# Decode attention over two caches: the last softmax maximum ahead of a PV product, and V stationary for B's last two PV products

## The chip, the cores and the metric

The kernel runs on one core of a Trainium2 chip. The metric is device microseconds of one execution, given as the median of several runs. Beside these runs there is one execution recorded by the hardware profiler; all durations of single instructions come from it.

## What is computed

Two independent attention blocks, A and B, each for one new token with 32 heads of 128 elements. A attends over its whole cache of 16384 positions, B only over the last 4096 positions of its cache. The two output rows of 512 are put side by side.

```python
q = (x @ wq).reshape(B, Sq, Hq, Dh)           # x: 1 x 512, 32 heads of 128
# B alone: k, v = the last W = 4096 positions of the caches
scores = jnp.einsum("bhqd,bhkd->bhqk", q, k) * (Dh ** -0.5)
p = _softmax(scores, axis=-1)
o = jnp.einsum("bhqk,bhkd->bhqd", p, v)
return o.transpose(0, 2, 1, 3).reshape(B, Sq, Hq * Dh) @ wo    # 4096 x 512
```

All inputs and the output are bf16. Every cached key and value is used once, by one query, so that nearly all of the traffic is K and V read once from HBM.

## The kernel before, in words

**Tiles and steps.** There are 20 steps T (`steps`, `NT`), 16 of A and 4 of B. The B steps are T = 0, 7, 13 and 19; step 18 is the last of A and step 19, the last of all, is B. An A step takes two heads: their 2 x 16384 positions lie on 128 partitions, 256 positions each. A B step takes eight heads as two groups of four, 128 positions on each partition for either group. Each step is walked in two halves, u = 0 and u = 1. For A a half is half of the positions of the pair, for B a half is a group of its own. A `Unit` is what has a softmax of its own: an A pair, or one B group.

**Scores.** These are made on VectorE, in place in the K tile: `scores_prod` (L194) multiplies K by the query, `scores_tree` halves the 128 products by additions (L201) and ends with a reduction (L207).

**Softmax.** `unit_max` takes a maximum on each partition (L212) and transposes it on TensorE (L214). `max_all` takes the maximum for each head on VectorE (L219, L223) and spreads it by a matmul (L226). `soft` makes the bias and the exponentials on ScalarE (L231, L234), the sums of the exponentials on TensorE (L241 or L246), and spreads the probabilities into `pm`, one masked copy for each head (L253). `recip` takes the reciprocal of the sums on VectorE. For a unit with `un.last` the sum comes out on all 128 partitions, with the heads as columns (L240, L241, L261), otherwise on a few rows (L246, L263).

**PV.** `pv` (L275) is 32 matmuls for a half: the probabilities are the stationary operand (128 x 8 for A, 128 x 16 for B), four positions of V, 512 elements, move past them. The result has 4 rows for each head, of which `evict` (L291, ScalarE) makes a scaled copy, `columns` (L306, eight matmuls) adds the four slices into columns, and L310 writes them to `s.O`. `pv_columns` (L317) does the same in another manner: V of one position is the stationary operand (128 x 128), the heads' probabilities move (4 columns), 128 matmuls in all, and the result is already in columns; one VectorE instruction (L321) scales it and writes `s.O`. Before the change only the last group, (19, 1), uses it.

**Output.** `permute_o` puts the 32 columns of O in the order of wo's rows, `project_out_columns` (L345) multiplies 128 blocks of wo, each stationary, by one column of O each, and `store_out` transposes, casts and stores. B's wo comes in five pieces of 16, 8, 4, 2 and 2 of its 32 row blocks (`wo_pieces`), and the products of a piece follow those of the one before.

**Queues and order.** The order on each engine is the order in which the code is written out. All loads of K, V and the weights go through SyncE's one DMA queue, in the order of the code, and a load whose tile is still read waits there. The V ring has two slots. At the end its tiles are V(18,0), V(18,1), V(19,0) and B's wo, so that B's wo takes the slot of V(18,1) and can be requested only when `pv(18, 1)` has read it. A's wo and V(19,1) share a slot of the K ring. At the last two turns of the loop, x = 38 and 39, and behind the loop the order is, in short:

```python
# x = 38: ... pv(17, 1); load_v(18, 1); pv(18, 0); scores_tree(19, 0) ... unit_max(19, 0)
# x = 39: load_v(19, 0); load_v(19, 1, W); columns(); scores_prod(19, 1)
#         max_all + soft of (19, 0); pv(18, 1); load_wo(B)
#         scores_tree(19, 1); recip; evict(); unit_max(19, 1)
# behind: columns(); max_all + soft + recip of (19, 1); pv(19, 0); evict(); columns()
#         permute_o(A); project_out_columns(A); store_out(A)
#         pv_columns(19, 1); permute_o(B); project_out_columns(B); store_out(B)
```

Of the kernel before, what the change touches and what calls it, by code (L numbers as in the profile page):

```python
# [10 lines left out]
BF16 = mybir.dt.bfloat16  # L11
P = 128
# [5 lines left out]
CH = 128  # L18
# [7 lines left out]
def kernel(  # L26
# [37 lines left out]
    def vslot(name):  # L64
        return vring.tile([P, CH, DH], BF16, tag="vring", name=name)
# [74 lines left out]
    def load_wo(s, W, pieces):  # L140
        s.wo_t = W.rearrange("p a b -> p (a b)").rearrange("p (r f) -> p r f", r=HQ)
        src = s.wo.rearrange("(p r) f -> p r f", r=HQ)
        r = 0
        for n in pieces:
            nc.sync.dma_start(out=s.wo_t[:, r : r + n, :], in_=src[:, r : r + n, :])
            r += n
# [31 lines left out]
    class Unit:  # L178
        def __init__(self, T, u):
            self.T = T  # L180
            self.s, g = steps[T]
            self.col = self.s.nh * g if self.s is A else self.s.nh * (2 * g + u)
            self.n = 2 * CH if self.s is A else CH
            self.rows = 4 * self.s.nh
            self.last = T == NT - 1 and u == 1
            self.sc = one.tile([P, 2 * CH], F32, tag="sc", name="sc")

    units = {}
# [39 lines left out]
    def soft(un):  # L228
        s = un.s
        bias = small.tile([P, 1], F32, tag="bias", name="bias")  # L230
        nc.scalar.activation(out=bias[:, :], in_=un.sm[:, 128:129], func=ACT.Copy, scale=-inv)  # L231
        p = one.tile([P, 2 * CH], BF16, tag="p", name="p")
        cs = small.tile([P, 1], F32, tag="cs", name="cs")
        nc.scalar.activation(  # L234
            out=p[:, 0 : un.n], in_=un.sc[:, 0 : un.n], func=ACT.Exp, scale=inv, bias=bias[:, :],
            accum_out=cs[:, :],
        )
        if un.last:
            csm = small.tile([P, 4], F32, tag="csm", name="csm")
            nc.scalar.activation(out=csm[:, 0 : s.nh], in_=s.mask[:, :], func=ACT.Copy, scale=cs[:, :])  # L240
            nc.tensor.matmul(  # L241
                un.sm[:, 136 : 136 + s.nh], lhsT=ones_col[:, :].broadcast_to([P, P]), rhs=csm[:, 0 : s.nh],
                start=True, stop=True,
            )
        else:
            nc.tensor.matmul(  # L246
                un.sm[0 : un.rows, 136:137], lhsT=s.rows[:, :, :].rearrange("p a b -> p (a b)"), rhs=cs[:, :],
                start=True, stop=True,
            )
        pm = small.tile([P, 4 * CH], BF16, tag="pm", name="pm")  # L250
        un.pm = pm[:, 0 : un.n * s.nh].rearrange("p (i h c) -> p i h c", h=s.nh, c=4)
        for j in range(s.nh):
            nc.scalar.activation(  # L253
                out=un.pm[:, :, j, :], in_=p[:, 0 : un.n].rearrange("p (i c) -> p i c", c=4),
                func=ACT.Copy, scale=s.mask[:, j : j + 1],
            )

    def recip(un):
        un.r = small.tile([P, 4], F32, tag="r", name="r")
        if un.last:  # L260
            nc.vector.reciprocal(un.r[:, 0 : un.s.nh], un.sm[:, 136 : 136 + un.s.nh])  # L261
        else:
            nc.vector.reciprocal(un.r[0 : un.rows, 0:1], un.sm[0 : un.rows, 136:137])  # L263
# [3 lines left out]
    def pv(T, u):  # L267
        s = steps[T][0]
        un = units[T, u if s is B else 0]
        first, final = (True, True) if s is B else (u == 0, u == 1)  # L270
        if first:
            un.o = ps_o.tile([16, 512], F32, tag="o", name="o")
        i0 = u * CH // 4 if s is A else 0
        for i in range(CH // 4):
            nc.tensor.matmul(  # L275
                un.o[0 : un.rows, :],
                lhsT=un.pm[:, i0 + i, :, :].rearrange("p a b -> p (a b)"),
                rhs=V[T, u][:, 4 * i : 4 * i + 4, :],
                start=(first and i == 0),
                stop=(final and i == CH // 4 - 1),  # L280
            )
        if final:
            ready.append(un)
# [3 lines left out]
    def evict():  # L287
        while ready:
            un = ready.pop(0)
            un.osb = one.tile([16, 512], F32, tag="o4", name="o4")  # L290
            nc.scalar.activation(  # L291
                out=un.osb[0 : un.rows, :], in_=un.o[0 : un.rows, :], func=ACT.Copy,
                scale=un.r[0 : un.rows, 0:1],
            )
            evicted.append(un)
            if ready:
                columns()

    def columns():
        while evicted:  # L300
            un = evicted.pop(0)
            s, n = un.s, un.rows
            oc = ps_s.tile([P, 4], F32, tag="sp", name="oc")
            sel = identf[0:n, 0:n].rearrange("k (h c) -> k c h", c=4)
            for j in range(4):
                nc.tensor.matmul(  # L306
                    oc[:, 0 : s.nh], lhsT=un.osb[0:n, j * P : (j + 1) * P], rhs=sel[:, j, :],
                    start=(j == 0), stop=(j == 3),
                )
            nc.scalar.copy(s.O[:, un.col : un.col + s.nh], oc[:, 0 : s.nh])  # L310

    def pv_columns(T, u):
        un = units[T, u]
        s = un.s
        o = ps_o.tile([P, 4], F32, tag="o", name="ocol")
        for l in range(CH):
            nc.tensor.matmul(  # L317
                o[:, 0 : s.nh], lhsT=V[T, u][:, l, :], rhs=un.pm[:, l // 4, :, l % 4],
                start=(l == 0), stop=(l == CH - 1),
            )  # L320
        nc.vector.tensor_tensor(  # L321
            out=s.O[:, un.col : un.col + s.nh], in0=o[:, 0 : s.nh], in1=un.r[:, 0 : s.nh], op=ALU.mult
        )
# [50 lines left out]
    with tc.manual_schedule():  # L374
        for s in (B, A):
            nc.scalar.dma_start(out=s.xT[:, :], in_=s.x[0, 0, :].rearrange("(p c) -> p c", c=KC))
        scratch = kslot("scratch")
        new_k(0)
        load_wq(B)
        load_k(0, 0)  # L380
        load_wq(A)
        load_k(0, 1)
        make_identity(nc, identf[:, :])
        nc.vector.memset(one_f[:, :], 1.0)
        nc.vector.memset(ones_col[:, :], 1.0)
        nc.vector.tensor_copy(ident[:, :], identf[:, :])
        spread_x(B, scratch[:, :, :].rearrange("p a b -> p (a b)"))
        for s in (B, A):
            make_masks(s)
        nc.vector.memset(pick[:, :], 0.0)  # L390
        nc.vector.tensor_copy(
            pick[:, 4 : 4 + P].rearrange("h (m k) -> h m k", k=4)[:, :, 0], identf[0:HQ, 0:HQ]
        )
        spread_x(A, one.tile([P, 2 * KC * P], BF16, tag="o4", name="xbA")[:, :])
        project_q(B)
        project_q(A)
        new_k(1)
        load_k(1)
        done = None
        for x in range(2 * NT):  # L400
            T, u = divmod(x, 2)
            if u == 0 and T >= 1:
                load_v(T - 1, 0)
                if T + 1 < NT:
                    new_k(T + 1)
                    load_k(T + 1)
            if x == 2 * NT - 2:
                W = kslot("wot")
                load_wo(A, W[:, 0:CH, :], (HQ,))
            if x == 2 * NT - 1:  # L410
                load_v(T, 0)
                load_v(T, 1, W[:, CH : 2 * CH, :])
            columns()
            scores_prod(T, u)
            if done is not None:
                max_all(done)
                soft(done)
            if u == 0 and T >= 1:
                if T >= 2:
                    pv(T - 2, 1)  # L420
                load_v(T - 1, 1)
                pv(T - 1, 0)
            if x == 2 * NT - 1:
                pv(T - 1, 1)
                load_wo(B, vslot("wot")[:, :, :], wo_pieces)
            nxt = scores_tree(T, u)
            if done is not None:
                recip(done)
            evict()
            done = nxt  # L430
            if done is not None:
                unit_max(done)
        columns()
        max_all(done)
        soft(done)
        recip(done)
        pv(NT - 1, 0)
        evict()
        columns()
        permute_o(A)  # L440
        project_out_columns(A, (HQ,))
        store_out(A)
        pv_columns(NT - 1, 1)
        permute_o(B)
        project_out_columns(B, wo_pieces)
        store_out(B)
# [30 lines left out]
```

## Time and profile before

| what | value |
|---|---|
| median of 3 runs | 836.62 us (834.75 to 836.89) |
| the profiled execution, its own time | 833.46 us |
| its span, first to last instruction | 831.7 us |
| mean granted TensorE clock | 0.704 |
| VectorE busy | 761.0 us (92%) |
| TensorE matmul busy | 394.2 us (47%) |
| ScalarE busy | 67.8 us (8%) |
| read from HBM | 352.32 MB, 424 GB/s over the span |

The span leaves out 1.76 us of the profiled execution's time that lies before its first and behind its last instruction. Positions such as "at 792.62" are microseconds from the start of the span. "Granted clock" is the share of TensorE's full speed that the throttle gave. In the tables of the profile, PE is TensorE's matmuls, PEld its weight loads, DVE is VectorE, ACT ScalarE, and SPq the DMA requests that SyncE issues; "issue" is time in which an engine waited for nothing that the profile shows.

### The profile page before, as it was taken

Reading aid. Unit: us, or ns where it says so; the run is one execution under the profiler, and the core shown is the slowest. Engines: PE = TensorE matmul, PEld = TensorE weight load, DVE = VectorE, ACT = ScalarE, POOL = GpSimd, SP = SyncE. Lnnn points to the kernel's source line nnn. Section 1 sums busy time; section 2 is a strip of 40 time slices with the busy share of each in tenths; the row PEclk is TensorE's granted clock in tenths of the full one; section 3 lists DMA queues with packets and bytes.
Section 4 is the critical chain, followed back from the end, with each engine's and each line's share of the span. In section 5 each row is a group of like instructions: output and inputs, shape, how many; then the busy total and the mean of one; then the engine's idle time right before and its main releaser. Section 6 shows DMA issues by size and latency. Waiting matters only on the chain.

```text
span 831.7 us, 4818 instructions
## 1 busy us (share of the span) xinstructions
PE 394.2 (47%) x2012; PEld 171.9 (21%) x2012; DVE 761.0 (92%) x356; ACT 67.8 (8%) x196; POOL 0.7 (0%) x6
## 2 busy tenths in 40 slices
PE   3515061808263453638081635536371808163677
PEld 1102020303021221213030212112120303021236
DVE  1899999999999999999999999999999999999910
ACT  0011010100000011101010000111010101000111
POOL 0000000000000000000000000000000000000000
PEclk9666576758585867667585958676676758595886
DMA  9999999999999999999999999999999999999994
GB/s 378 429 435 461 409 455 405 450 419 432 448 414 432 428 448 416 442 426 439 424 443 419 445 421 430 442 422 445 418 449 416 442 424 444 416 432 432 430 426 173
DMA packets 10694, 352.64 MB, mean 424 GB/s; under 512 B 1456, under 2 KB 1456, under 8 KB 1840
## 3 DMA queue, kind: packets, MB, share of 16 engines
q1 hardware_dynamic: 10376, 352.33, 98.4%
q8 instruction: 16, 0.26, 0.1%
q10 hardware_dynamic: 296, 0.00, 0.0%
q14 instruction: 6, 0.05, 0.0%
HBM read 352.32 MB, written 0.00 MB: 424 GB/s over the span
## 4 chain that ended last, share of the span: by engine, by line
DVE 79%; DMA 15%; PE 5%; issue 1%; ACT 1%; DVEq 0%; ACTq 0%
DVE kt L194 36%; DVE kt L201 35%; DMA kt<-in_A_k_cache_dram 10%; DVE sc L207 5%; PE o L275 3%; DMA xTA<-in_A_x_dram 3%; DMA vt<-in_A_v_cache_dram 2%; PE out_cols L345 1%; DVE m L212 1%; DVE Mr L223 1%; DVE M L219 0%; PE ocol L317 0%; PE oc L306 0%; ACT o L291 0%; DVE r L263 0%
## 5 line engine op out<-in xcount | busy, mean ns | idle before, releaser
L201 DVE TENSOR_TENSOR kt<-kt 128x8192 bf16<-128x8192 bf16 (+3 forms) x160 | 344.9, 2156 | 4.7
L275 PE MATMUL o<-vt,pm 128*8 128x512 bf16 (+1 forms) x1248 | 316.0, 420 | 9.9 <-DMA vt<-in_A_v_cache_dram 9.9
L194 DVE TENSOR_TENSOR kt<-kt,qA 128x16384 bf16<-128x16384 bf16 x32 | 277.5, 8672 | 2.9 <-DMA kt<-in_A_k_cache_dram 2.9
L275 PEld LDWEIGHTS <-pm 128*8 128x8 bf16 (+1 forms) x1248 | 116.2, 94 | 199.8 <-issue 72.5
L214 PE MATMUL sm<-identf,m 128*1 128x128 f32 x24 | 8.4, 350 | 196.5 <-DVE m L212 196.4
L226 PE MATMUL sm<-one_f,Mr 1*128 1x1 f32 x48 | 13.1, 340 | 177.4 <-DVE Mr L223 177.4
L194 DVE TENSOR_TENSOR kt<-kt,qB 128x16384 bf16<-128x16384 bf16 x8 | 69.5, 8681 | 0.0
L207 DVE TENSOR_REDUCE sc<-kt 128x128 f32<-128x1024 bf16 x40 | 48.8, 1220 | 2.9
L226 PEld LDWEIGHTS sm<-one_f,Mr 1*128 1x128 f32 x48 | 11.1, 286 | 183.9 <-DVE Mr L223 183.9
L214 PEld LDWEIGHTS sm<-identf,m 128*1 128x1 f32 x24 | 1.9, 80 | 199.8 <-issue 191.1
L231 ACT ACTIVATE bias<-sm 128x1 f32<-128x1 f32 x24 | 4.1, 171 | 387.2 <-PE sm L226 387.1
L291 ACT ACTIVATE o<-o,r 8x512 f32<-8x512 f32 (+1 forms) x23 | 15.6, 678 | 183.1 <-PE o L275 183.1
L306 PE MATMUL oc<-identf,o 8*128 8x2 f32 (+1 forms) x184 | 24.5, 252 | 3.7 <-ACT o L291 3.7
L306 PEld LDWEIGHTS oc<-identf,o 8*128 8x128 f32 (+1 forms) x184 | 22.5, 189 | 12.0 <-issue 6.5
L321 DVE TENSOR_TENSOR OB<-ocol,r 128x4 bf16<-128x4 f32 x1 | 0.2, 162 | 17.8 <-PE ocol L317 17.8
L172 PE MATMUL qp<-wqt,scratch 128*128 128x512 bf16 x32 | 9.5, 470 | 13.7 <-DVE scratch L161 13.7
L219 DVE TENSOR_REDUCE M<-sm 1x2 f32<-1x128 f32 (+1 forms) x24 | 6.5, 271 | 10.2 <-PE sm L214 10.2
L172 PE MATMUL qp<-wqt,xbA 128*128 128x512 bf16 x32 | 10.0, 488 | 10.0 <-DMA wqt<-in_A_wq_dram 10.0
L253 ACT ACTIVATE pm<-p,maskA 128x256 bf16<-128x256 bf16 x32 | 14.5, 500 | 0.5
L310 ACT CAST OA<-oc 128x2 bf16<-128x2 f32 x16 | 2.6, 160 | 110.2 <-PE oc L306 110.2
L234 ACT ACTIVATE p<-sc,bias 128x256 bf16<-128x256 f32 (+1 forms) x24 | 11.3, 472 | 0.8
L161 DVE COPY scratch<-xTB 128x128 bf16<-128x128 bf16 x4 | 0.7, 315 | 10.7 <-DMA xTB<-in_B_x_dram 10.7
(57 smaller groups left out, 84.4 us busy)
## 6 DMA issues: line engine op xcount, KB each, us to landing
vt<-in_A_v_cache_dram SPq DMA_DIRECT2D x32, 4096.0 KB, 26.4
kt<-in_B_k_cache_dram SPq DMA_DIRECT2D x8, 4096.0 KB, 30.1
vt<-in_B_v_cache_dram SPq DMA_DIRECT2D x7, 4096.0 KB, 30.0
wqt<-in_B_wq_dram SPq DMA_DIRECT2D x1, 4096.0 KB, 12.4
wqt<-in_A_wq_dram SPq DMA_DIRECT2D x1, 4096.0 KB, 31.2
wot<-in_A_wo_dram SPq DMA_DIRECT2D x1, 4096.0 KB, 30.2
wot<-in_B_v_cache_dram SPq DMA_DIRECT2D x1, 4096.0 KB, 30.8
wot<-in_B_wo_dram SPq DMA_DIRECT2D x1, 2048.0 KB, 15.1
```

The source lines that it names most:

```text
L172: nc.tensor.matmul(qp[:, :, :], lhsT=s.xb[:, j, c, :], rhs=wq[:, c, j, g : g + 4, :], start=(k == 0), stop=(k == n - 1),)
L194: nc.vector.tensor_tensor(out=k, in0=k, in1=s.q[:, j : j + 1, :].broadcast_to([P, CH, DH]), op=ALU.mult)
L201: nc.vector.tensor_tensor(out=k[:, :, 0:w], in0=k[:, :, 0:w], in1=k[:, :, w : 2 * w], op=ALU.add)
L207: nc.vector.tensor_reduce(out=un.sc[:, c0 : c0 + CH], in_=k[:, :, 0:8], axis=AX.X, op=ALU.add)
L212: nc.vector.tensor_reduce(out=m[:, :], in_=un.sc[:, 0 : un.n], axis=AX.X, op=ALU.max)
L214: nc.tensor.transpose(un.sm[0:1, 0:P], m[:, :], identf[:, :])
L226: nc.tensor.matmul(un.sm[:, 128:129], lhsT=Mr[:, :], rhs=one_f[:, :], start=True, stop=True)
L234: nc.scalar.activation(out=p[:, 0 : un.n], in_=un.sc[:, 0 : un.n], func=ACT.Exp, scale=inv, bias=bias[:, :], accum_out=cs[:, :],)
L253: nc.scalar.activation(out=un.pm[:, :, j, :], in_=p[:, 0 : un.n].rearrange("p (i c) -> p i c", c=4), func=ACT.Copy, scale=s.mask[:, j : j ...
L275: nc.tensor.matmul(un.o[0 : un.rows, :], lhsT=un.pm[:, i0 + i, :, :].rearrange("p a b -> p (a b)"), rhs=V[T, u][:, 4 * i : 4 * i + 4, :], ...
L291: nc.scalar.activation(out=un.osb[0 : un.rows, :], in_=un.o[0 : un.rows, :], func=ACT.Copy, scale=un.r[0 : un.rows, 0:1],)
L306: nc.tensor.matmul(oc[:, 0 : s.nh], lhsT=un.osb[0:n, j * P : (j + 1) * P], rhs=sel[:, j, :], start=(j == 0), stop=(j == 3),)
```

## The change

`soft` is split. The matmul for the sums, and for a last unit the small ScalarE instruction in front of it, move behind the `pm` copies into a new function `soft_sum`. In the loop `soft_sum` is called directly behind `soft`. Behind the loop, `pv(18, 1)` and the requests for B's wo, which stood in turn x = 39, stand between `soft` and `soft_sum` of the last group. Both groups of the last step are now `un.last`, and (19, 0) goes through `pv_columns` in place of `pv`, `evict` and `columns`. The only unit that is still evicted behind the loop is A's last pair; its `columns` stands behind `pv_columns(19, 0)`.

```diff
-            self.last = T == NT - 1 and u == 1
+            self.last = T == NT - 1
...
+        un.cs = cs
+        pm = small.tile([P, 4 * CH], BF16, tag="pm", name="pm")
+        un.pm = pm[:, 0 : un.n * s.nh].rearrange("p (i h c) -> p i h c", h=s.nh, c=4)
+        for j in range(s.nh):
+            nc.scalar.activation(
+                out=un.pm[:, :, j, :], in_=p[:, 0 : un.n].rearrange("p (i c) -> p i c", c=4),
+                func=ACT.Copy, scale=s.mask[:, j : j + 1],
+            )
+
+    def soft_sum(un):
+        s, cs = un.s, un.cs
         if un.last:
             csm = small.tile([P, 4], F32, tag="csm", name="csm")
             nc.scalar.activation(out=csm[:, 0 : s.nh], in_=s.mask[:, :], func=ACT.Copy, scale=cs[:, :])
...
-        pm = small.tile([P, 4 * CH], BF16, tag="pm", name="pm")
...
                 max_all(done)
                 soft(done)
+                soft_sum(done)
             if u == 0 and T >= 1:
                 if T >= 2:
                     pv(T - 2, 1)
                 load_v(T - 1, 1)
                 pv(T - 1, 0)
-            if x == 2 * NT - 1:
-                pv(T - 1, 1)
-                load_wo(B, vslot("wot")[:, :, :], wo_pieces)
             nxt = scores_tree(T, u)
...
         columns()
         max_all(done)
         soft(done)
+        pv(NT - 2, 1)
+        load_wo(B, vslot("wot")[:, :, :], wo_pieces)
+        soft_sum(done)
         recip(done)
-        pv(NT - 1, 0)
         evict()
+        pv_columns(NT - 1, 0)
         columns()
         permute_o(A)
         project_out_columns(A, (HQ,))
```

More of the change, by code (lines that the diff above doesn't have):

```diff
@@ L248, in soft @@
                 start=True, stop=True,
-            )
-        pm = small.tile([P, 4 * CH], BF16, tag="pm", name="pm")
[L251 to L255, printed above, removed]
             )
```

## The prediction

> **What bounds the kernel now.** I read the page first (slices, DMA issues), then the chain of waits in order of time over the last 110 us, the waits of that stretch, its timeline, and a table of the DMA share in short stretches. From the page:
>
> ```profile
> DMA  9999999999999999999999999999999999999994
> ...
> vt<-in_A_v_cache_dram SPq DMA_DIRECT2D x32, 4096.0 KB, 26.4
> ...
> wot<-in_B_v_cache_dram SPq DMA_DIRECT2D x1, 4096.0 KB, 30.8
> wot<-in_B_wo_dram SPq DMA_DIRECT2D x1, 2048.0 KB, 15.1
> wot<-in_B_wo_dram SPq DMA_DIRECT2D x1, 1024.0 KB, 17.2
> wot<-in_B_wo_dram SPq DMA_DIRECT2D x1, 512.0 KB, 18.0
> wot<-in_B_wo_dram SPq DMA_DIRECT2D x2, 256.0 KB, 18.3
> ```
>
> Until the last slice the DMA engines are full, so the change can only act in the last 40 us. The last numbers are us from request to landing. The chain of waits there:
>
> ```profile
> 773.70 18.88 DMA vt<-in_A_v_cache_dram
> 792.58 0.04 issue
> 792.62 9.16 PE o L275 x32
> 801.78 0.02 issue
> 801.81 0.69 ACT o L291
> ...
> 804.93 0.39 PE sm L241 x2
> 805.31 7.02 PE o L275 x32
> 812.33 0.02 issue
> 812.35 0.69 ACT o L291
> 813.04 0.04 issue
> 813.08 1.06 PE oc L306 x8
> ...
> 815.15 3.36 PE out_cols L345 x126
> 818.52 0.60 issue
> ...
> 824.75 3.57 PE out_cols L345 x128
> ```
>
> From the landing of V(18,1) at 792.58 to the end it is one chain on TensorE, with short steps of ScalarE between. It is not the DMA: V(19,1) lands at 781.20+30.8 = 812.0 and is used at 819.72; B's wo, requested from 801.80 to 803.6, lands at 816.9, 819.5, 820.7, 821.3 and 821.9 and is used from 824.75. What makes the chain long stands in the waits:
>
> ```profile
> DVE M L219 <- PE sm L214: 10.2, 1, 10.2
> PE o L275 <- DMA vt<-in_A_v_cache_dram: 9.7, 1, 9.7
> ```
>
> The last group's partition maximum (L212) is there at 791.50+0.29 = 791.79, but its transpose (L214) is queued on TensorE behind `pv(18, 1)`, which waits 9.7 us for V and then works 9.16. So the last softmax begins at 801.70, when TensorE has nothing else to do: 3.5 us pass from the end of `pv(18, 1)` (801.78) to the start of `pv(19, 0)` (805.24).
>
> **The change part by part.**
>
> *Maximum ahead of `pv(18, 1)`.* With L214 in front, the steps follow m's end by gaps of the trace: m to L214 0.15 us (at 753), L214 to L219 0.31 and to L223 another 0.31 (at 801.7), L223 to L226 0.34 and 0.36 of L226 (at 781), or 0.58 at the granted clock of 0.50 that stands there (row at 762). That is 791.94, 792.25, 792.56, 792.90 and an end at 793.3 to 793.5. The product now starts behind that, at 793.4 in place of 792.62: **+0.8 us**, the one new wait on the path. Behind it on TensorE stand `pv(18, 1)` and all that follows, and SyncE's requests for wo. It is 0 if V comes later than 793.4, and grows one for one if VectorE is late. `pv(18, 1)` itself had ten slow matmuls (0.43 us each) before the clock rose from 0.50 to 1.00 at about 797; I keep 9.14 us, so it ends at 802.55 (802.1 if the clock rises at the same moment as before).
>
> *Softmax of the last group.* Bias, exponentials, four copies into `pm` and the small L240 take 0.17+0.40+0.19+1.26+0.30 us on ScalarE. They now run from 793.5 to 796, under the 9 us of `pv(18, 1)`; without that cover they would cost 2.3 us. Only L241, 0.39 us, stands between the two products. The stretch of 3.5 us becomes 0.4: **-3.05 us** (802.95).
>
> *`pv_columns(19, 0)` for `pv(19, 0)`.* The old 32 matmuls take 7.07 us. The new ones have the shape of L317, which is in the trace:
>
> ```profile
> 819.72 3.60 PE L317 MATMUL ocol<-pm,wot 128*128 128x4 bf16 x128
> ```
>
> That is 28 ns from one to the next: **-3.45 us** (806.55). L317 ran at a granted clock of 0.50; L345, the same stationary shape, gave 126 in 3.36 us, 27 ns, where the clock was between 1.00 and 0.50, so the clock does not decide. Each weight load's own row is 104 ns, and they overlap.
>
> [...] The trace has 104 ns as a duration and 28 ns as the spacing, so I take the spacing.
>
> V(19,0) must have landed: it lies between V(18,1) (792.6) and V(19,1) (812.0) with equal bytes, so about 802.3, just ahead of 802.95. Its landing has no row; it was there at 805.24 at the latest, so the wait is between 0 and 2.3 us, and I take 0 by the even spacing.
>
> *Eviction.* B's group loses its eviction (0.68) and columns from the end; A's pair takes its place. A's L291 runs on ScalarE under `pv_columns(19, 0)`. On TensorE remain eight L306 (1.05 us), then L310, and now `permute_o(A)` waits for A's column. From the scaling that precedes `permute_o` to the first L345 it took 823.36 to 824.75 = 1.39 us for B; I take this. 1.05+0.03+1.39 = 2.5 us for 2.84 (812.31 to 815.15): **-0.35 us**; A's projection starts at 809.1. The added scaling on VectorE, L321 of (19, 0), 0.16 us, meets an idle engine and is used only at 817.
>
> *B's wo.* Its five requests move 0.8 us later on SyncE's queue, to 802.6 to 804.4; only the output's store is behind them. The queue is then still busy with V(19,0) and V(19,1) until 812.0, and 2 MB, 1 MB and 0.5 MB land 4.9, 2.6 and 1.2 us after one another, some 430 GB/s as in the slices of the page. So the landing stays at 821.9 and the delay is free up to some 8 us; a gain isn't to be had either, since the bytes in front are the same. The tail of the transfer:
>
> ```profile
> 820.00:821.00 1.00, 1.00 (x44) 1.00 (x42) 0.00 (x0) 0.22 (x1) 0.00 (x0) 0.50 0.43 160
> 821.00:822.00 1.00, 1.00 (x44) 1.00 (x41) 0.00 (x0) 0.00 (x0) 0.00 (x0) 0.50 0.06 22
> ```
>
> Columns: stretch, length, busy of PE, PEld, DVE, ACT, POOL, clock, DMA share, GB/s. The transfers end in the last row.
>
> *`soft_sum` in the loop, `last` for (19, 0).* L246 keeps its place on TensorE; for (19, 0) L241 waits some 1.6 us longer for ScalarE, and the next instruction on TensorE is L214 at 792. 0.
>
> *Instruction supply.* TensorE has 192 more instructions (128 pairs for 32). The only trace of a cost is the hole of 0.60 us ("issue") inside A's projection, at full DMA; an instruction packet had begun at 816.5. The two column runs after it, with the DMA draining, had none. Three runs (`pv_columns(19, 0)`, A's projection, `pv_columns(19, 1)`) now lie under full DMA: 0 to 3 such holes. One is in the sum; the bounds are -0.6 and +1.2. [...]
>
> *Sum.* A's projection 809.1 + 4.15 (815.15 to 819.30, with the hole) = 813.25; 0.42 to the next product, 3.60: 817.3; 1.39 to B's projection: 818.7. It takes 3.56: 822.25. By pieces: the last piece's eight matmuls may start at 821.9 at the earliest, end 822.1. So TensorE and the DMA come out nearly level, and **any further gain on TensorE would be wo's wait**. Against 828.31 that is 0.8-3.05-3.45-0.35 = **-6.05, say -6.0 us**. The tail behind it is unchanged (3.4 us). Span 831.7 to 825.7, the profiled execution 833.46 to 827.5. The median of the runs is 3.2 us above that execution; I put the same 6.0 on it: 836.62 to **830.6**.
>
> **Rivals.**
>
> 1. *A smaller gain, instruction supply.* Holes of 0.6 us in all column runs, or longer ones since the DMA is full there, and a late V(19,0): 1.2 + 2.3 us at the worst, gain 2.5 to 5, 832 to 834. For it: the hole at 818.52. Against: between the runs lie 2.5 and 0.4 us in which TensorE takes few instructions, and two of the three column runs of before had no hole.
>
> 2. *wo is last, no change.* If the later request lands later in full, or the drain under 0.5 share (820 to 822) stretches, B's projection waits. For no measurable change (under 0.3%, 2.5 us, about what a measurement of this kernel can tell) the last piece must land after 825.4, 3.5 us late; 834 to 839. The requests' 0.8 us don't reach that.
>
> 3. *Slower: VectorE behind V.* The maximum is now ahead of `pv(18, 1)`, so if the scores of (19, 1) end late, the product, the requests and all of the chain wait one for one. In the trace the scores end 0.8 us before V lands; before the change they had 10 us. It decides when m ends 6 us later, at 798; with 10 us more it costs 4 us, 840. Against: every L194 and L201 group from 714.9 on takes 8.7 us, without a hole over 0.1 us. A spacing of 104 ns in `pv_columns(19, 0)` would end on the same side (13.3 us for 3.6, +3.7 in all), but L317 excludes it.
>
> 4. *The change doesn't do what it says*: L214 still waits behind V. The gain is then what `pv_columns` and the eviction bring, 3.8 us less 0 for the start: 832.8. Nothing in the code's order says so.
>
> **How the numbers follow.** The forecast (gain 5 to 6.5) has 0.78; rival 1 0.10, rival 4 0.02, both faster; rival 2 0.05; rival 3 0.05. So faster 0.90, same 0.05, slower 0.05. The range runs from the profiled execution's base with the full gain (827.5) to the highest run less 3 us (833.9), which takes in most of rivals 1 and 4 and leaves out rivals 2 and 3.
>
> **What would show it.** Right: L214 at 792 with no 10 us wait in front of L219; `pv(18, 1)` from about 793.4, directly behind L226; L241 and then 128 L317 within 4.1 us behind it; L345 of A at 809; B's projection ending within 0.5 us of wo's last landing; end of span 6 us sooner. Wrong: a wait of L275 for V unlike 792.6, DMA waits in front of L317, holes over 1 us in the column runs, or L345 of B waiting over 1 us for wo.

## The result, and the profile after

The changed kernel takes 830.01 us (median of 6 runs, 829.73 to 830.10) against 835.64 us before (6 runs, 833.28 to 836.89). The ratio is 0.9935, 95% interval 0.9919 to 0.9951. In a second comparison it was 830.29 us and 0.9937 (0.9922 to 0.9952). These ratios, here and below, go by the means of the runs, not by their medians. The profiled execution is 829.86 us with a span of 828.1 us; before it was 833.46 and 831.7. So the medians moved by 5.6 us and the two profiled executions by only 3.6 us, and both numbers need an explanation.

The page of the changed kernel, slices of the DMA and its requests (last column: us from request to landing):

```profile
DMA  9999999999999999999999999999999999999995
...
wot<-in_B_v_cache_dram SPq DMA_DIRECT2D x1, 4096.0 KB, 31.1
wot<-in_B_wo_dram SPq DMA_DIRECT2D x1, 2048.0 KB, 14.3
```

The DMA is full as before. The requests for wo are issued from 802.58 to 804.8, and its last piece still lands at about 821.8. The chain of waits of the changed kernel, its end (L279 is now `pv`, L252 the sums, L321 `pv_columns`, L310 `columns`, L349 the projection):

```profile
791.72 0.14 issue
791.86 0.38 PE sm L214
...
792.90 0.58 PE sm L226 x2
793.48 9.07 PE o L279 x32
802.55 0.32 PE sm L252 x2
802.86 3.22 PE ocol L321 x128
806.09 0.99 PE oc L310 x8
...
808.43 1.15 PE out_cols L349 x38
809.58 0.03 issue
809.61 2.55 PE out_cols L349 x90
...
812.77 0.96 PE ocol L321 x37
813.74 2.07 issue
815.81 2.58 PE ocol L321 x91
...
819.80 0.99 PE out_cols L349 x32
820.80 1.21 issue
822.01 2.71 PE out_cols L349 x96
```

And the waits of the changed kernel that stand where 10.2 and 9.7 us stood:

```profile
PE ocol L321 <- issue: 2.1, 1, 2.1
PE out_cols L349 <- issue: 1.2, 1, 1.2
DVE M L219 <- PE sm L214: 0.6, 1, 0.6
```

The transpose L214 runs as soon as the maximum is there, the last softmax lies under `pv(18, 1)`, and the column products follow directly. What is new are two holes of 2.07 and 1.21 us on TensorE in which it waits for nothing that the profile shows. The positions on the path, in us from the start of the span:

| position | before | predicted | after | moved |
|---|---|---|---|---|
| `pv(18, 1)` starts | 792.62 | 793.4 | 793.48 | +0.86 |
| first product of (19, 0) | 805.31 | 802.95 | 802.86 | -2.45 |
| its end | 812.33 | 806.55 | 806.09 | -6.24 |
| A's projection starts | 815.15 | 809.1 | 808.43 | -6.72 |
| `pv_columns(19, 1)` ends | 823.34 | 817.3 | 818.39 | -4.95 |
| B's projection starts | 824.75 | 818.7 | 819.80 | -4.95 |
| B's projection ends | 828.32 | 822.25 | 824.72 | -3.60 |

Up to A's projection the change brings more than was forecast. Behind that the holes cost 3.3 us, where the kernel before lost 0.60 in this way: a net loss of 2.7 us. A second profile of the changed kernel (`after_again`) has holes at the same three places, of 0.20, 1.80 and 1.21 us.

### The profile page after: what moved, and what is told of

Its sections match the earlier page's. It is cut to its first block, busy times and chain, and to the rows that moved or that the text cites. A ratio compares the mean times of both kernels' runs of the same rounds, so it can differ in the third digit from the quotient of the medians.

```text
span 828.1 us, 4994 instructions
## 1 busy us (share of the span) xinstructions
PE 387.3 (47%) x2100; PEld 171.3 (21%) x2100; DVE 761.4 (92%) x357; ACT 67.2 (8%) x195; POOL 0.7 (0%) x6
## 4 chain that ended last, share of the span: by engine, by line
DVE 80%; DMA 15%; PE 3%; issue 1%; SPq 0%; ACT 0%; DVEq 0%
DVE kt L201 36%; DVE kt L194 36%; DMA kt<-in_A_k_cache_dram 10%; DVE sc L207 5%; DMA kt<-in_B_k_cache_dram 5%; PE o L279 1%; PE out_cols L349 1%; DVE m L212 1%; PE ocol L321 1%; DVE Mr L223 1%; DVE M L219 1%; DVE r L267 0%; SPq L135 0%; PE oc L310 0%; PE out_rows L367 0%
## 5 line engine op out<-in xcount | busy, mean ns | idle before, releaser
L279 PE MATMUL o<-vt,pm 128*8 128x512 bf16 (+1 forms) x1216 | 306.7, 419 | 1.2 <-DMA vt<-in_A_v_cache_dram 1.2
L279 PEld LDWEIGHTS <-pm 128*8 128x8 bf16 (+1 forms) x1216 | 112.8, 94 | 185.4 <-issue 60.6
L214 PE MATMUL sm<-identf,m 128*1 128x128 f32 x24 | 8.5, 354 | 206.6 <-DVE m L212 206.6
L214 PEld LDWEIGHTS sm<-identf,m 128*1 128x1 f32 x24 | 1.9, 79 | 209.6 <-issue 200.8
L310 PE MATMUL oc<-identf,o 8*128 8x2 f32 (+1 forms) x176 | 23.1, 249 | 2.4 <-ACT o L295 2.4
L310 PEld LDWEIGHTS oc<-identf,o 8*128 8x128 f32 (+1 forms) x176 | 21.2, 186 | 10.0 <-issue 6.5
L242 ACT ACTIVATE pm<-p,maskB 128x128 bf16<-128x128 bf16 x32 | 10.2, 390 | 0.3
L257 PE MATMUL sm<-cs,rowsA 128*8 128x1 f32 x32 | 3.1, 167 | 14.3 <-ACT p L234 14.3
```

The costliest lines, as they stand in the source:

```text
L214: nc.tensor.transpose(un.sm[0:1, 0:P], m[:, :], identf[:, :])
L242: nc.scalar.activation(out=un.pm[:, :, j, :], in_=p[:, 0 : un.n].rearrange("p (i c) -> p i c", c=4), func=ACT.Copy, scale=s.mask[:, j : j ...
L279: nc.tensor.matmul(un.o[0 : un.rows, :], lhsT=un.pm[:, i0 + i, :, :].rearrange("p a b -> p (a b)"), rhs=V[T, u][:, 4 * i : 4 * i + 4, :], ...
L310: nc.tensor.matmul(oc[:, 0 : s.nh], lhsT=un.osb[0:n, j * P : (j + 1) * P], rhs=sel[:, j, :], start=(j == 0), stop=(j == 3),)
```

## The experiments

The theory after the result has two parts. First, the holes are TensorE's supply with instructions. A pair is a weight load and its matmul, two instructions; a column run is 128 such pairs in a row, as `pv_columns` and `project_out_columns` have them. From the hole at 813.74 to the one at 820.80 TensorE executes 91 pairs of L321, one pair of L331, four of L336 and 32 of L349, which is 128 pairs or 256 instructions. From the small hole at 809.58 to the one at 813.74 there are 90 pairs, one of L367 and 37, again 256. Such a block of 256 instructions is called a page below. The table of DMA queues fits: for 2100 matmuls and as many weight loads the changed kernel has 16 packets of 16 KB on an instruction queue (`q8 instruction: 16, 0.26, 0.1%`), one for about 260 instructions. Second, the runs of the kernel before differ among themselves by something that the change removes. The rivals are that the holes belong to those places in the code or to the rate of the pairs, and that the spread comes from the landing of the data.

**The two parts of the change by themselves.** `max_only` keeps the order of the change, but (19, 0) is computed in the old way. It needs two evictions behind one another.

```diff
-            self.last = T == NT - 1
+            self.last = T == NT - 1 and u == 1
...
         evict()
-        pv_columns(NT - 1, 0)
+        pv(NT - 1, 0)
         columns()
+        evict()
+        columns()
```

> The last maximum and softmax ahead of pv(18, 1) as in the change, but (19, 0) by pv, evict and columns as before. A's last eviction and columns now stand behind pv(19, 0) and add 1.05 us to the path. Sum: +0.8 for the later start, -3.05 for the softmax under pv(18, 1), +1.05: B's projection ends 1.2 us sooner than before, at 827.1; about 834.5 us. If the maximum were the main part of the change, it would be 830 to 831.

Measured: 832.64 us (832.43 to 833.10) beside 834.20 of the kernel before, ratio 0.9977 (0.9965 to 0.9988). Its chain of waits:

```profile
803.07 7.00 PE o L279 x32
810.08 0.99 PE oc L310 x8
...
811.25 0.58 ACT o L295
811.87 1.06 PE oc L310 x8
...
817.38 0.57 issue
```

The old product starts at 803.07, as the new one does in the change, so the softmax is hidden; but it takes 7.00 us, and both columns (0.99 and 1.06) and one eviction stand behind it. The projection of B ends at 827.45 (expected 827.1). The time was 1.9 us below the expected 834.5, since that was set against the first median, 836.62. The holes are small here, 0.57 and 0.14 us.

`cols_only` does the reverse: `pv(18, 1)` and the requests for wo stand at x = 39 again, (19, 0) goes through `pv_columns`.

```diff
+            if x == 2 * NT - 1:
+                pv(T - 1, 1)
+                load_wo(B, vslot("wot")[:, :, :], wo_pieces)
             nxt = scores_tree(T, u)
...
-        pv(NT - 2, 1)
-        load_wo(B, vslot("wot")[:, :, :], wo_pieces)
         soft_sum(done)
         recip(done)
-        evict()
         pv_columns(NT - 1, 0)
-        columns()
```

> (19, 0) by pv_columns, but the last maximum, pv(18, 1) and the requests for wo in the order of before. By durations alone: -3.45 for the product and -1.75 for the eviction and columns that no unit needs any more behind it, so -5.2: the projection of B ends at 823.1. By the theory that TensorE's instructions come in pages of 256 and that a page takes about 6 us while the DMA is full: holes of about 2 us each in A's projection and in pv_columns(19, 1), and the end at about 826.4, 2 us sooner than before.

Measured: 831.91 us (831.31 to 833.17), ratio 0.9969 (0.9956 to 0.9981). Its chain of waits:

```profile
806.82 0.59 PE sm L252 x2
807.40 3.41 PE ocol L321 x128
...
813.07 1.01 issue
...
818.21 2.07 issue
```

The two holes are there, 1.01 and 2.07 us, after 38 pairs of A's projection and 37 of `pv_columns(19, 1)`, and B's projection begins at 824.27, only 0.5 us before that of the kernel before. It ends at 827.84, not at the expected 826.4; this execution (832.99 us) was among the slowest of the 12, with `pv(18, 1)` at 9.63 us. One cost I had not expected: in the split `soft` the small ScalarE step for the sums stands behind the four `pm` copies, so L252 starts 1.55 us after the exponentials' end at 805.27, where L241 started 0.38 us after it (804.93 against 804.55). In the full change that lies under `pv(18, 1)` and costs nothing, so `cols_only` pays 1.2 us that the change doesn't. Neither half brings what both bring together: the lower runs of the kernel before are at 833.3, from which the halves gain about 0.7 and 1.4 us and the whole 3.3.

**The DMA taken away from the end.** `quiet_dma` leaves out the loads of V(19,1) and of B's wo; V(19,0) and A's wo are used in their place, so it computes something else.

```diff
-                load_v(T, 1, W[:, CH : 2 * CH, :])
+                V[T, 1] = V[T, 0]
...
-        load_wo(B, vslot("wot")[:, :, :], wo_pieces)
+        B.wo_t = A.wo_t
```

> The changed kernel without the loads of V(19,1) and of B's wo: V(19,0) and A's wo are used twice, so the DMA is idle from about 802 on. Theory (a page of TensorE's instructions waits behind the data while the DMA is full): no hole over 0.3 us in the column runs, the projection of B ends at about 821.4 in place of 824.7, the span 3.3 us shorter. Rival (the holes come from TensorE's own queue or from the pairs' rate): the same 2.07 and 1.21 us at the same places, the span unchanged.

Measured: 825.95 us (825.52 to 827.67). The three column runs behind (19, 0) in its chain of waits are whole:

```profile
810.08 3.57 PE out_cols L349 x128
...
814.26 3.40 PE ocol L321 x128
...
819.07 3.57 PE out_cols L349 x128
```

No hole is over 0.15 us, at a DMA share of 0.00 to 0.04 between 802 and 809. So the rate of the pairs alone does not make the holes; here, with the DMA idle, they are gone. B's projection ends at 822.64, not at 821.4. This execution, the slowest of the four (827.67 us), had `pv(18, 1)` at 9.63 us and `columns` at 1.81 us for 0.99 to 1.06; the granted clock stood at 0.50 from 806 on, where its mean between 806 and 808 was still 0.97 in the change. V(19,0), whose landing had no row in the profile before, is seen here, with no load behind it: 780.39 + 22.0 = 802.4.

**Boundaries moved.** `pad80` and `pad48` are the changed kernel with 80 and 48 unused pairs of a weight load and a one-column matmul in TensorE's idle time after 784.

```diff
                 soft_sum(done)
+                if x == 2 * NT - 1:
+                    for _ in range(80):  # or 48
+                        nc.tensor.matmul(
+                            done.sm[:, 200:201], lhsT=ident[:, :], rhs=ident[:, 0:1], start=True, stop=True
+                        )
```

> The changed kernel once more, beside the kernels of this comparison: 829.7 to 830.2 us, with holes of about 2.1 us after 37 matmuls of pv_columns(19, 1) and 1.2 us after 32 of B's projection.

> The changed kernel with 80 idle pairs of weight load and 1-column matmul (160 instructions, results unused) in TensorE's idle time before 791. Theory (pages of 256 instructions, about 6.2 us from entering one to having the next while the DMA is full): each boundary moves 80 pairs earlier, so it falls after pair 86 of A's projection, after 85 of pv_columns(19, 1) and after 80 of B's. Holes of about 0.6 and 2.1 us and none in B's projection, which then ends at about 824.0 in place of 824.7: 829.2 us. Rival (holes belong to places in the code): they stay after 37 and 32, time unchanged.

> The same with 48 pairs (96 instructions). Theory: the boundaries fall after pair 3 of pv_columns(19, 0), in A's columns (L310) behind it, near pair 118 of A's projection and of pv_columns(19, 1), with holes of about 2.5, 0.8 and 2.1 us; B's projection ends at 825.5 to 826.8 and the kernel is 1 to 2 us slower than the change alone: 831 to 832. Rival: time unchanged, holes after 37 and 32.

Measured in one comparison: the change alone 830.29 us (829.87 to 830.49), `pad80` 829.00 (828.65 to 829.68), `pad48` 828.88 (828.18 to 829.37). The chain of waits of `pad80`:

```profile
808.58 2.44 PE out_cols L349 x86
811.01 0.24 issue
811.26 1.28 PE out_cols L349 x42
...
813.15 2.25 PE ocol L321 x85
815.40 2.06 issue
817.46 1.30 PE ocol L321 x43
...
820.17 3.57 PE out_cols L349 x128
```

and of `pad48`:

```profile
808.01 3.29 PE out_cols L349 x118
811.29 0.73 issue
...
813.05 3.10 PE ocol L321 x117
816.15 2.07 issue
...
820.08 3.57 PE out_cols L349 x128
```

Every boundary moved by exactly the number of pairs put in: from 38 to 86 and from 37 to 85 with 80 (48 later is 80 earlier, modulo 128), from 38 to 118 and from 37 to 117 with 48. That is the page theory to the pair, and it excludes the places in the code. In both kernels the next boundary, 80 or 112 pairs into B's projection (at about 822.4 and 823.2), falls where the DMA has drained (at most 10 GB/s from 822 on), and B's projection is whole; both run about 1.3 us below the change, with no overlap of their runs with its own. They are the fastest versions here that compute the result: 0.9923 (0.9907 to 0.9939) and 0.9921 (0.9905 to 0.9937) of the kernel before. In the profile of `pad80` the holes account for the gain: they add up to 2.30 us for 3.31, and B's projection ends 0.98 us sooner. In `pad48` they account for half of it: they add up to 2.80 us, and 0.4 us of the 1.07 by which B's projection ends sooner come from `pv(18, 1)`, which began 0.1 us sooner and took 8.75 us for 9.07 (the clock between 797 and 798 was 1.00 for 0.68). Since that product took 8.45 to 9.85 us in four profiles of the kernel before, it is not shown that the pairs made it faster. For `pad48` I had expected a loss; that was wrong. The early boundary, after pair 3 of `pv_columns(19, 0)`, brought no hole. The next instruction packet began between 802.0 and 802.5, about when that pair ran (802.4), though in the change it begins 3.2 to 3.9 us after a page is entered (next paragraph). My estimate from these two times is that the page was entered some 3 us ahead of the matmuls that TensorE was working on, during the slow `pv(18, 1)`; I had let it be entered only with the matmul itself. No run tests this.

How long a page takes: in the changed kernel the page after 809.6 is to be had at 815.81, the one after 815.81 at 822.01, 6.2 us each (6.2 also in `pad80`, `pad48` and `cols_only`, from the end of one hole to the end of the next; 5.9 and 6.2 in `after_again`), and the instruction packets begin 3.2 to 3.9 us after the entry (in the half microseconds from 813.0 and 819.0). After 822.01, with the DMA drained, the packet begins 1.0 to 1.5 us after the entry, from 823.0 on. The DMA share was 0.97 to 1.01 from 809.6 to 815.8, 0.76 from there to 820.8, and 0.08 between 821 and 822. A column run of 128 pairs takes 3.2 to 3.6 us, so three of them in a row ask for pages faster than these come: 2.07 us of the wait for the first of the two pages were open, and 1.21 us of the wait for the second.

**Smaller rows.** Does the instruction packet wait behind long rows? `small_rows` loads V(19,0) and V(19,1) in eight transfers each and B's wo in rows of at most 4 KB; `pad48_small` has this and the 48 pairs.

```diff
-        nc.sync.dma_start(out=V[T, u][:, :, :].rearrange("p l d -> p (l d)"), in_=src)
+        flat = V[T, u][:, :, :].rearrange("p l d -> p (l d)")
+        if T == NT - 1:
+            w = CH * DH // 8
+            for c in range(8):
+                nc.sync.dma_start(out=flat[:, c * w : (c + 1) * w], in_=src[:, :, c * w : (c + 1) * w])
+        else:
+            nc.sync.dma_start(out=flat, in_=src)
...
-            nc.sync.dma_start(out=s.wo_t[:, r : r + n, :], in_=src[:, r : r + n, :])
+            m = min(n, 4) if s is B else n
+            for k in range(r, r + n, m):
+                nc.sync.dma_start(out=s.wo_t[:, k : k + m, :], in_=src[:, k : k + m, :])
```

> The changed kernel with V(19,0) and V(19,1) loaded in eight transfers each (4 KB per partition in place of 32 KB) and B's wo in rows of at most 4 KB, same bytes, same order. Theory A (an instruction page waits behind whole rows already queued on its DMA engine): the 6.2 us from entering a page to having the next shrink towards the 3 us seen when the DMA is idle, the holes of 2.07 and 1.21 us fall below 0.5 us each, B's projection waits for wo's last landing at 821.8 at most; 827.5 to 828.5 us. Theory B (it waits for a share of the bytes, whatever their rows): holes and time as in the change, 829.9 to 830.5.

> The same small rows together with the 48 unused pairs, which alone gave 828.88 with holes of 0.73 and 2.07 us. Theory A: no hole left, 827.5 us, bound by wo's last landing near 821.8 plus eight matmuls. Theory B: as with the pairs alone, 828.9.

Measured: 832.73 us (832.06 to 833.89) and 832.05 us (831.77 to 832.39), 2.4 and 3.2 us above the same kernels with long rows in the comparison before. From the waits of SyncE's queue and the timeline of `small_rows` (the bracket is the idle time in front of the row), and the row of the same hole in `after_again`, the changed kernel with long rows:

```profile
SPq L153 <- DMA out_dram<-rows: 8.3, 1, 8.3
...
814.78 2.56 PE L329 MATMUL ocol<-pm,wot 128*128 128x4 bf16 x91 [1.78 <-issue]
```

```profile
815.82 2.56 PE L321 MATMUL ocol<-pm,wot 128*128 128x4 bf16 x91 [1.80 <-issue]
```

Two things follow. While the DMA was still full (a share of 0.94 between 810 and 814, 0.47 in the next 2 us), the hole after 37 pairs of `pv_columns(19, 1)` was 1.78 us, for 2.07 and 1.80 in the two profiles with long rows. So there is no sign that short rows help; theory A is not supported. Its 3 us for an idle DMA were my estimate; `quiet_dma` shows only that a page was there within 4.1 us of the one before (estimated from the spacing of its pairs: from pair 39 of A's projection, at 811.14, to pair 38 of `pv_columns(19, 1)`, at 815.24, with no hole at either). `pad48_small` has no hole, which theory A expected, but it can't tell: `pv(18, 1)` and `columns` were slower there (9.39 and 1.81 us), so that the first page had more time, and the DMA share was down to 0.51 and 0.34 between 814 and 818, where the second fell. And the further requests for wo waited, by the profile's reading, for earlier transfers, one of them for 8.3 us for A's output store, so that the DMA share fell to 0.34 between 816 and 818 and more than half of wo came in after 819, its last piece at about 826.7. B's projection then waited for wo for 4.0 us. This was not the experiment I meant to make, but it shows the price of a late request for wo, which the change itself stays clear of. Why those requests waited for unrelated transfers was not tried.

**The spread of the kernel before.** Over the first two comparisons of experiments and the first runs it has 64 times: 25 from 836.3 to 837.0, none between 835.0 and 836.3, and below that 21 under 834.0 and 18 above. I call them the upper, the lower and the middle group. The median of the kernel before in a comparison depends on how many runs of each it has: 834.20, 836.40 and 836.36 us in the three comparisons of experiments. Three more executions of the unchanged kernel were profiled.

> The kernel before, unchanged, to see its own spread (833.3 to 836.9 us so far) and where it lies. Theory: the spread lies in the last 60 us, in holes of TensorE's instruction supply (0.60 us in the first profile, inside A's projection); a second profile that differs by 1 us or more shows it as a longer hole in L345 or L317, or as a later V(18,1) (792.6 before). Rival: it lies in the 790 us in front, as a later landing of K or V; then all rows from 715 on are shifted alike and the tail from V(18,1)'s landing to the end is 39.1 us as in the first profile.

> The kernel before once more, for one profile. If it falls in the upper group (836.4 to 837.0), the theory of the clock expects pv(19, 0) at 10.4 us (two windows of 3.4 us at a granted clock of 0.50) in place of 7.07, and V and wo landing as before; in the middle group 8.7 us, in the lower 7.07.

> The same, a further profile: 7.07, 8.7 or 10.4 us for pv(19, 0) in the lower, middle and upper group, with the start of B's projection later by the same amount.

`before_again` was profiled in the middle group (834.67 us, 12 runs with a median of 834.27), `before_c` (836.75) and `before_d` (836.53) in the upper. From the chain of waits of `before_again`, and its granted clock (third column from the end) in a stretch:

```profile
804.69 8.71 PE o L275 x32
```

```profile
806.00:809.00 3.00, 3.00 (x8) 0.96 (x7) 0.00 (x0) 0.00 (x0) 0.00 (x0) 0.50 0.99 426
```

The same two views of `before_c`:

```profile
805.94 9.67 PE o L275 x32
```

```profile
804.50:811.50 7.00, 6.15 (x16) 2.34 (x17) 0.18 (x1) 1.93 (x7) 0.00 (x0) 0.52 0.97 417
```

`pv(19, 0)` takes 7.02 us in the lower group (the first profile), 8.71 in the middle, 9.67 and, in `before_d`, 9.86 in the upper. The first theory, longer holes in the instruction supply, failed: the hole in A's projection is 0.60 us in `before_again` as in the first profile, 0.38 in `before_c`, and `before_d` has none. V(18,1) is used at 792.71, 792.72 and 792.56, as in the first profile (792.62), and wo has landed by about 822 in all of them, where it is used from 825.95 at the earliest. So the data are not it. What differs is the granted clock: it falls to 0.50 for about 3.4 us in the middle group and for about 6.8 us in the upper, in the last 1.5 us of the 3.5 us in which TensorE had little to do or up to 1.1 us behind them. The expected 10.4 us for the upper group was too much: there the clock fell 1.5 and 1.1 us ahead of the product, so that 5.3 and 5.7 us of the slow stretch lay in it. Half of 3.4, 5.3 and 5.7 us is what the product lost in the three profiles (1.7, 2.65 and 2.84). The longer fall, 6.8 us, is twice the shorter; what sets these lengths is not shown. TensorE was busy for about half of the gap (in `before_c` 1.05, 0.24 and 0.59 us of the 3.73 between the two products), and in the first profile, with 1.05, 0.24 and 0.39 of 3.53 us, the clock stayed at 1.00, so how little work lets the clock fall is not shown either. In the upper group `pv(18, 1)` is also slower (9.49 in `before_c` and 9.85 in `before_d` for 9.16) and so is L241 (0.59 for 0.39); in `before_c` the three together, 2.65 + 0.33 + 0.20, make 3.2 us, as much as B's projection starts later (827.95 for 824.75; the other differences nearly cancel). `keep_warm` puts work into that gap:

```diff
+        fill = ps_t.tile([P, 4, DH], F32, tag="tp", name="fill")
+
+        def warm(n):
+            for _ in range(n):
+                nc.tensor.matmul(fill[:, :, :], lhsT=ident[:, :], rhs=B.q[:, 0:4, :], start=True, stop=True)
+
+        warm(3)
         columns()
         max_all(done)
+        warm(4)
         soft(done)
```

> The kernel before with 3 and 4 unused matmuls of 512 columns in TensorE's idle time between pv(18, 1) and pv(19, 0), while it waits for ScalarE. Theory: the runs of the kernel before fall in three groups (about 833.3, 834.5 and 836.7) because in that stretch of 3.5 us TensorE does little, and in some runs the granted clock falls to 0.50 for one or two windows of 3.4 us in pv(19, 0) (8.76 us for 7.07 in the second profile). With TensorE busy the clock stays at 1.00: all runs at 833 to 834, the spread under 1 us. Rival (the groups come from the landing of V or wo): the spread of 3.6 us stays.

Measured: 832.98 us, all 12 runs from 832.53 to 833.78, beside 836.40 of the kernel before (833.22 to 836.86); ratio 0.9971 (0.9960 to 0.9982). Its chain of waits has the old length of the product, and its granted clock stays at 1.00:

```profile
805.54 7.02 PE o L275 x32
```

```profile
808.00:810.00 2.00, 2.00 (x11) 0.81 (x9) 0.00 (x0) 0.00 (x0) 0.00 (x0) 1.00 0.86 369
```

The upper two groups are gone. The spread was 1.3 us where 1 was expected. Seven unused matmuls make the kernel before 3.4 us shorter by the median of this comparison; against the lower group it is some 0.3 us. The unused matmuls also move the page boundaries (A's projection has no hole here, for 0.60), but that is too little for groups 1.2 to 3.4 us apart. And `max_only` shows the same without any unused work: it keeps the old product, has no gap in front of it, runs it in 7.00 us at a clock of 1.00, and its 12 runs lie within 0.7 us.

## Why the prediction was right, and where it was not

The forecast was a gain of 6.0 us to 830.6, with a range from 827.5 to 833.9; the median is 830.01. The direction holds, and so does the mechanism up to A's projection. But the profiled execution gained 3.6 us and not 6.0, and the number is as near as it is because two errors of similar size lie on opposite sides: 2.7 us of holes, and a base that was 3.2 us above the profiled execution. That is luck.

*Maximum ahead of the product.* As forecast: L214 at 791.86, `pv(18, 1)` at 793.48 for 793.4, its end at 802.55 for 802.55. That the end is met exactly is luck too: the clock rose at another moment in each execution (from 795.5 to 798.2 in the four profiles of the kernel before), and the same product took 9.16, 8.45, 9.49 and 9.85 us there.

*Softmax.* The stretch between the products is 0.31 us for the forecast 0.4. `max_only` shows it alone.

*`pv_columns(19, 0)`.* The chain gives 128 pairs in 3.22 us, 25 ns apart, at a granted clock of 1.00, where 3.60 were forecast. That figure came from a row of the timeline; there the row is now

```profile
802.72 3.36 PE L321 MATMUL ocol<-pm,vt 128*128 128x4 bf16 x128
```

Like with like it is 3.36 for 3.60 us in the timeline and 3.22 for 3.41 in the chain. So the clock does decide a little, some 0.2 us, and the text said that it did not; the rest of the 0.4 is that a row of the timeline begins before the work ahead of it has ended (802.72 where the chain has 802.86). One weight load behind the other, at the 104 ns of a load's own row in the trace before, is excluded as a spacing here too. No wait for V(19,0) is seen; its landing in `quiet_dma`, 802.4, is 0.5 us ahead of its use here.

*Eviction.* 2.34 us for 2.5.

*wo.* Its last landing did not move, as forecast (821.8 for 821.9). It was not the bound in the end, since the holes came first; with them reduced in `pad48`, B's projection ended at 823.65, still about 1.8 us behind wo. The forecast that TensorE and the DMA come out nearly level did not hold: in the change it is 2.9 us (824.72 against 821.8).

*Instruction supply.* This is the step that failed. I saw the one hole of 0.60 us, took holes of that size as the unit and put +1.2 us as the upper bound. Measured: 0.03, 2.07 and 1.21 in place of 0.60, a loss of 2.7 us. Holes over 1 us in the column runs were among the prediction's own signs of being wrong. The number of runs under full DMA was counted rightly, but the size was not. The spacing of the instruction packets in the trace before (they begin in the half microseconds from 816.5, 820.0 and 823.5) gives no warning, since a column run takes 3.6 us. The hole itself does: 256 instructions before its end lie the four pairs of L332, at 814.63 to 814.89, so that page was there only 4.2 to 4.5 us after TensorE had begun the one before it, and a column run uses one up in 3.6. With three such runs in a row under full DMA the holes then grow; the 6.2 us could not be read from that trace.

*The base.* The profiled execution was forecast at 827.5 and is 829.86, 2.4 us off, for that reason. The median was forecast by taking the same 6.0 us from 836.62, 3.2 us above the profiled execution, without asking what those 3.2 us were. They were the upper group, mainly `pv(19, 0)` at a lowered clock. The change puts the products directly behind one another and replaces the one that the clock slows (7.0 to 9.9 us) by one that it hardly slows (3.22 us at 1.00, 3.41 at 0.50); its runs lie within 0.4 us. The first of the two is enough for that, as `max_only` shows. Against the lower group the change gains 3.3 us, against the upper 6.6, and the median in between depends on how often the clock fell.

*The rivals.* The first, a smaller gain through instruction supply and a late V, had the holes right; V was not late. The profiled execution's 3.6 us lie in its range of 2.5 to 5; its time, 832 to 834, was not reached because the base of 836.62 was that of the upper group. wo as the bound and VectorE behind V did not occur: the maximum was there at 791.72, before 792.6, where V was used in the kernel before.

## What to carry to other kernels

Ask not only when an operand is there but what is queued in front of its user: a transpose of 0.3 us behind a product that waited 9.7 us for data cost a whole softmax here, 3.5 us for 0.31 between the products. Before many short pairs replace a few long matmuls, count instructions, and compare the time in which they use up a block with the time that a block takes to come in the trace, above all where the DMA is full (here 3.2 to 3.6 us against 5.9 to 6.2); 80 unused pairs in idle time earlier were worth 1.3 us here, though that holds only for this very program. And when the profiled execution and the median differ by several times the runs' agreement, find out what the runs differ in before an edit is priced against either.

## What the runs showed of the hardware that was not expected

- From one hole to the next TensorE executed 256 instructions, in the change, `pad80` and `pad48` alike, and the ends of two holes lay 5.9 to 6.2 us apart (in the change at a DMA share of 0.97 to 1.01 in the first of these stretches, and falling to 0.08 in the second). With the DMA idle (`quiet_dma`) no hole was over 0.15 us. With 4 KB rows in the queue the hole was 1.78 us, for 2.07 and 1.80 without.
- Around the end of a gap of 3.5 us with little work the granted clock fell to 0.50 in three of the four profiled executions of the kernel before, for 3.4 or 6.8 us, at 1.7 to 2.8 us of the following product's time. With the gap filled (`keep_warm`) or gone (`max_only`) it stayed at 1.00.
- Column products with 128 columns stationary ran at 25 ns a pair at a clock of 1.00 (3.22 us for 128) and 27 ns at 0.50 (3.41 us), where a product of 32 matmuls of 512 columns went from 7.0 to 9.9 us with only part of it at 0.50.
